# The maximum over 128 partitions taken on TensorE and VectorE instead of GpSimd, in a sparse attention with a mixture of experts

## The chip, the cores and the metric

The kernel runs on one core of a Trainium2 chip. A core has TensorE (PE in the profile, with its weight loads as PEld), VectorE (DVE), ScalarE (ACT), GpSimd (POOL) and SyncE (SP, which here issues most DMAs). Data lies in SBUF, in 128 partitions; TensorE writes to PSUM, of 8 banks. The metric is the device time of one execution in microseconds, as the median of several runs.

## The reference

First a block-sparse attention for 4 batches, 8 heads, 768 positions and a head dimension of 64, then eight dense experts over the 3072 rows of 512 that come out of it, mixed by a matrix `P` that is normalised eight times over its rows and its columns. Cut to what matters:

```python
scores = np.where(mask, scale * q @ k.T, -1e9)       # mask by blocks of 32
attn = softmax(scores)
x = (attn @ v)  -> (3072, 512)

logits = x @ w_gate                                   # (3072, 8)
logits = logits - logits.max()                        # one maximum over all
P = np.exp(logits)
for _ in range(8):
    P /= P.sum(1, keepdims=True) + 1e-09
    P /= P.sum(0, keepdims=True) + 1e-09
    P *= N / E
for e in range(8):
    h = np.maximum(x @ w1[e], 0.0)                    # (512 x 1024)
    out += P[:, e:e+1] * (h @ w2[e])                  # (1024 x 512)
```

## The kernel before

**Numbers in two halves.** TensorE multiplies float16 here. Each float32 operand of an expert's product is split into a high and a low float16 part, and three products (high by low, low by high, high by high) are added up. Before the split an operand is multiplied by a power of two, made from the largest absolute value of the whole tensor. That maximum lies over all 128 partitions: VectorE first reduces each partition to one number, then the 128 numbers are reduced to one that every partition needs. The second step is the GpSimd library call `partition_all_reduce` (PARTITION_ALL_REDUCE in the profile). It is called for the gate's weights and for v of each batch (`pow2_scale`, L120), for w1 and w2 of each of the eight experts (`scale_steps`, L177), and for the maximum of the logits (`weigh`, L897).

**Attention.** The program text walks over 192 tiles of 128 rows (`T`). For each it makes scores (L510, L513), adds the mask and takes the row maximum (L518), exponentiates (L523), splits the result in two halves (L532, L536; some on POOL), has a DMA turn it (`pt<-ph`, L558), and four tile pairs later multiplies by v (L577, into one of two PSUM banks called "pm", which one head's sums hold for six tiles). v is loaded, scaled and split per batch. The first expert's w1 is scaled in this stage too.

**Experts.** A step `i` is one expert and one batch, 32 in all. `stage1(i, qi)` makes a quarter of the hidden layer by a scheme of seven block products instead of eight (L945, into one of four banks "ph"); DVE combines the products (L955), ACT and POOL form sums (`add`, L1010 to L1022, with four POOL pieces at L1017 and L843), and the results are split into `h` (ACT L965, DVE or POOL L975). `stage2(i, p)` multiplies by w2 (L1058, into four banks "py") and DVE adds to the output (L1079). Step `i`'s second stage and step `i + 1`'s first alternate on PE.

**A new expert.** When the last batch of an expert is at work, the next expert's w1 is split into seven operands (ACT L821, DVE L825), with sums of its blocks formed on POOL (L836). Only then is the one raw buffer `r` free, and w2 is loaded into it (2 MB, L156), scanned for its maximum in eight parts (`part`, L170), reduced (`whole`, L176), passed to the library call (L177), turned into a scale (`power`, L180 to L185), and split, again with sums on POOL (L836). One batch later the w1 of the expert after that is loaded and scanned in the same way.

**What sets the order.** A class `Slots` holds these side jobs in the program text: urgent ones and a lazy list, the latter strictly in its order. After each product PE is given, `tick` advances the clock of the list by one and takes the next jobs that are due and that fit beside PE by their costs. `scale_w` puts the eight parts, `whole` and `power` on the lazy list:

```python
slots.add(whole, key, 1, True, dve=0.1)
slots.add(power, key, 2, True, dve=0.5)
```

The text's order is not the last word: at build time the instructions of all engines are ordered again by a model of their times, so that the scan of the first w1, for instance, which the text has at tile 101 of 192, runs 118 us after the start. Each engine then works through its own queue in order.

Of the kernel before, what the change touches and what calls it, by code (L numbers as in the profile page):

```python
# [8 lines left out]

# [1 line left out]
F32 = mybir.dt.float32  # L11
# [5 lines left out]
ALU = mybir.AluOpType  # L17
AX = mybir.AxisListType
PSUM = bass.MemoryType.PSUM

P = 128
# [25 lines left out]
TW = 100  # L47
# [12 lines left out]
def tile_sparse_attention_moe(  # L60
# [11 lines left out]
    nc = tc.nc  # L72
    B, H, S, D = q.shape
    NT, DM = out.shape
    NE, _, FF = w1.shape
# [20 lines left out]
    ident = const.tile([P, P], F32, name="ident")  # L96
# [3 lines left out]
    lg = const.tile([P, NTT, NE], F32, name="lg")  # L100
# [6 lines left out]
    dram = ctx.enter_context(tc.tile_pool(name="dram", bufs=1, space=bass.MemoryType.DRAM))  # L107
    xd = [dram.tile([P, NP, 2, KH, TH], F16, name=f"xd_{b}") for b in range(B)]

    def pow2_scale(srcs, s, inv, tag):  # L110
        m = small.tile([P, len(srcs)], F32, tag="mx", name=f"mx_{tag}")
        for i, src in enumerate(srcs):
            nc.vector.tensor_reduce(
                out=m[:, i : i + 1], in_=src, axis=AX.X, op=ALU.max, apply_absolute_value=True
            )
        if len(srcs) > 1:
            nc.vector.tensor_reduce(out=m[:, 0:1], in_=m, axis=AX.X, op=ALU.max)
        m = m[:, 0:1]
        a = small.tile([P, 1], F32, tag="ma", name=f"ma_{tag}")
        nc.gpsimd.partition_all_reduce(a, m, P, ReduceOp.max)  # L120
        nc.vector.tensor_scalar(a, a, TINY, HUGE, ALU.max, ALU.min)
        ai = a.bitcast(I32)
        nc.vector.tensor_scalar(ai, ai, 0x7F800000, None, ALU.bitwise_and)
        nc.vector.reciprocal(s, a)
        nc.vector.tensor_scalar(s, s, TOP, None, ALU.mult)
        nc.vector.tensor_scalar(inv, a, 1.0 / TOP, None, ALU.mult)
# [23 lines left out]
    wr = {}  # L150
# [5 lines left out]
        nc.sync.dma_start(out=t, in_=src[e].rearrange("(c p) f -> p c f", p=P))  # L156
        wr[which] = t

    def scale_steps(which, e, vector=nc.vector, gpsimd=nc.gpsimd):
        flat = wr[which].rearrange("p c f -> p (c f)")  # L160
        n = 8
        w = KD * FF // n
        m = small.tile([P, n], F32, tag="mx", name=f"mx_w{which}_{e}")
        a = small.tile([P, 1], F32, tag="ma", name=f"ma_w{which}_{e}")
        s = small.tile([P, 1], F32, tag=f"sw{which}", name=f"sw{which}_{e}")
        inv = small.tile([P, 1], F32, tag=f"iw{which}", name=f"iw{which}_{e}")
        wr["s", which], wr["i", which, e] = s, inv

        def part(k):
            vector.tensor_reduce(  # L170
                out=m[:, k : k + 1], in_=flat[:, k * w : (k + 1) * w], axis=AX.X,
                op=ALU.max, apply_absolute_value=True,
            )

        def whole():
            vector.tensor_reduce(out=a, in_=m, axis=AX.X, op=ALU.max)  # L176
            gpsimd.partition_all_reduce(a, a, P, ReduceOp.max)  # L177

        def power():
            vector.tensor_scalar(a, a, TINY, HUGE, ALU.max, ALU.min)  # L180
            ai = a.bitcast(I32)
            vector.tensor_scalar(ai, ai, 0x7F800000, None, ALU.bitwise_and)
            vector.reciprocal(s, a)
            vector.tensor_scalar(s, s, TOP, None, ALU.mult)
            vector.tensor_scalar(inv, a, 1.0 / TOP, None, ALU.mult)  # L185

        return [lambda k=k: part(k) for k in range(n)], whole, power

    KB = 1024
    w1p = {  # L190
# [127 lines left out]
    with ExitStack() as actx:  # L318
# [18 lines left out]
        with tc.tile_pool(name="mk", bufs=1, side="right") as mk:  # L337
            sbi = mk.tile([P, NB * NR], I64, name="sbi")
            nc.scalar.dma_start(
                out=sbi[R],  # L340
# [23 lines left out]
                out=sb[R],  # L364
# [51 lines left out]
        ps_t = pool("ps_t", 2, space=PSUM)  # L416
        ps_m = pool("ps_m", 2, space=PSUM)
        bank = [lambda nm: ps_m.tile([P, 512], F32, tag="pm", name=nm)]

        qscale = 1.0 / 8.0  # L420
        LDQ = (nc.sync, nc.gpsimd, nc.scalar)[QSEL]
# [216 lines left out]
        parts = {}  # L638
        ready, rest = first_steps()
        for T in range(NTILE + 4):  # L640
            if T < NTILE:
                parts[T] = front(T)
                if T + 1 < NC:
                    lay_mask(T + 1)
            if 0 <= T - LHI < NTILE:
                split_hi(T - LHI, *parts[T - LHI])
            if 0 <= T - LLO < NTILE:
                split_lo(T - LLO, *parts.pop(T - LLO))
                if (T - LLO) % G == G - 1:
                    transposes((T - LLO) // G)  # L650
            if T >= NTILE:
                continue
            if T // G >= LAG and T < NTILE and T % G == VPOS:
                for ci in range(G):
                    values(T // G - LAG, ci)
            n, c = divmod(T, NC)
            b, h = divmod(n, H)
            if n % 2 == 0 and c == CL and n // 2 + 2 < B * NHP:
                load_qk(*divmod(n // 2 + 2, NHP))
            if T == 20:  # L660
                split_gate()
            if T == 1:
                prep_q(1)
            if T == 2:
                prep_k(1)
                vsplit[0] = scale_v(0)
            if T in (3, 4, 5, 6):
                split_v(2 * T - 6, *vsplit[0])
            if todo and T % 3 == 0:
                todo.pop(0)()  # L670
            while ready and ready[0][0] <= T:
                ready.pop(0)[1]()
                if T % 2 == 0:
                    break
            if T == TW:
                load_w(1, 0)
                parts_w, whole_w, power_w = scale_steps(1, 0)
            if T - TW in range(1, 9):
                parts_w[T - TW - 1]()
            if T == TW + 10:  # L680
                whole_w()
            if T == TW + 12:
                power_w()
            if T < NTILE:
                if n + AHEAD < B * H:
                    if c == CQ:
                        prep_q(n + AHEAD)
                    if c == CK:
                        prep_k(n + AHEAD)
                if b + 1 < B:  # L690
                    if (h, c) == (2, 0):
                        load_v(b + 1)
                    if (h, c) == (3, 5):
                        vsplit[b + 1] = scale_v(b + 1)
                    if h >= 4 and c == 5:
                        split_v(2 * (h - 4), *vsplit[b + 1])
# [47 lines left out]
    ]  # L744
    accs = {b: big.tile([P, NC, DM], F32, name=f"acc_{b}") for b in range(B // 2)}
    bank[0] = lambda nm: ps_y.tile([P, 512], F32, tag="py", name=nm)

    def acc(t):
        return accs[t // NC][:, t % NC]
# [8 lines left out]
    class Slots:  # L758
        def __init__(self):
            self.now, self.pe, self.busy = 0, 0.0, [0.0, 0.0, 0.0]  # L760
            self.urgent, self.lazy = [], []

        def add(self, fn, key, delay=1, lazy=False, dve=0.0, act=0.0, pool=0.0):
            queue = self.lazy if lazy else self.urgent
            queue.append((fn, key, self.now + delay, (dve, act, pool)))

        def charge(self, costs):
            self.busy = [x + c for x, c in zip(self.busy, costs)]

        def run(self, queue, n):  # L770
            fn, _, _, costs = queue.pop(n)
            self.charge(costs)
            fn()

# [6 lines left out]
        def tick(self, pe, dve, act=0.0):  # L781
            self.now += 1
            self.pe += pe
            self.busy = [max(x, self.pe - lag) for x, lag in zip(self.busy, LAGS)]
            self.charge((dve, act, 0.0))
            n, held = 0, set()
            while n < len(self.urgent):
                _, key, ready, costs = self.urgent[n]
                if key not in held and ready <= self.now and self.fits(costs):
                    self.run(self.urgent, n)  # L790
                    n, held = 0, set()
                    continue
                held.add(key)
                if key[0][0] == "sum":
                    held.update((("h", key[1], p),) + key[1:] for p in (2, 4, 5, 6))
                n += 1
            while self.lazy and self.lazy[0][2] <= self.now and self.fits(self.lazy[0][3]):
                self.run(self.lazy, 0)

        def settle(self, i, qi):  # L800
            while any(x[1][1:] <= (i, qi) for x in self.urgent):
# [6 lines left out]

    slots = Slots()
    def scale_w(which, e):  # L810
        parts, whole, power = scale_steps(which, e, Pinned.vector, Pinned.gpsimd)
        key = ("scale", which, e)
        for k, part in enumerate(parts):
            slots.add(part, key, 6 if k == 0 else 1, True, dve=0.6)
        slots.add(whole, key, 1, True, dve=0.1)
        slots.add(power, key, 2, True, dve=0.5)

    def queue_split(dst, src, key, delay=1):
        s = wr["s", 1 if key[0] == "w1" else 2]
# [69 lines left out]
    def balance():  # L889
# [4 lines left out]

        def weigh():
            nc.vector.tensor_reduce(out=m, in_=flat(lg), axis=AX.X, op=ALU.max)
            nc.gpsimd.partition_all_reduce(m, m, P, ReduceOp.max)  # L897
            nc.vector.tensor_scalar(m, m, -1.0, None, ALU.mult)
            nc.scalar.activation(flat(pw), flat(lg), AF.Exp, bias=m)

# [304 lines left out]
```

## Time and profile before

| | |
|---|---|
| median of 3 runs | 2617.84 us |
| lowest and highest run | 2589.72 and 2622.93 us |
| the profiled execution | 2589.72 us, span 2589.7 us |
| attention | from 0 to some 612 us |
| first w2 loaded from | 606.9 us |
| later loads of w2 | 873.8, 1121.7, 1363.3, 1605.1, 1847.5, 2090.0, 2332.6 us |
| library calls | 22: 16 for w1 and w2, 4 for v, 1 for the gate, 1 for the logits |

The profiled execution is the lowest of the three. The loads of w2 mark the experts: from one to the next is an expert's period, 242 to 248 us. A profile row names the line and engine, what is written and read by the program's names, and how often; rows of the timeline begin with start and length in microseconds and end with the idle time before, and with the instruction that ended it. "Waits" rows give the total, the number of times and the longest.

### The profile page before, as it was taken

How to read it: one execution, taken by the hardware profiler on the slowest of the kernel's cores; microseconds unless marked ns; L12 is line 12 of the kernel's file. 1: busy time of each engine (PE TensorE's matmuls, PEld its weight loads, DVE VectorE, ACT ScalarE, POOL GpSimd, SP SyncE). 2: the span in 40 equal slices, each digit the busy share in tenths (PEclk: the TensorE clock that was granted, in tenths of full speed). 3: DMA queues.
4: the chain of work that ended last, by engine and by line, in shares of the span. 5: the costliest groups of instructions: out<-in, count | busy, mean ns of one | idle time of the engine just before them, and what ended most of it. 6: DMA issues, size and time to landing. Idle time of an engine off the chain costs nothing.

```text
span 2589.7 us, 46975 instructions
## 1 busy us (share of the span) xinstructions
PE 2361.4 (91%) x18270; PEld 1678.2 (65%) x18270; DVE 2009.5 (78%) x3747; ACT 1277.7 (49%) x2234; POOL 1559.8 (60%) x1387
## 2 busy tenths in 40 slices
PE   6999999897879979998998999899989998998999
PEld 3656666564656657765775677577657765776777
DVE  6768788675767788788778878877887788778876
ACT  4466767664445544444454444444444444444442
POOL 4557687763754476457556655755476557556653
PEclk9967879787989989999999999999999999999999
DMA  5679999996111221122121212211221122121211
GB/s 167 141 154 190 190 186 197 182 203 134 58 68 44 76 76 44 44 76 76 48 82 62 87 47 76 76 44 44 76 76 44 44 76 76 57 73 60 84 68 50
DMA packets 363924, 236.38 MB, mean 91 GB/s; under 512 B 303772, under 2 KB 316084, under 8 KB 363700
## 3 DMA queue, kind: packets, MB, share of 16 engines
q1 hardware_dynamic: 362128, 230.59, 34.9%
q10 hardware_dynamic: 1572, 2.78, 0.6%
q8 instruction: 143, 2.34, 0.4%
q14 instruction: 81, 0.66, 0.1%
HBM read 140.54 MB, written 17.30 MB: 61 GB/s over the span
## 4 chain that ended last, share of the span: by engine, by line
PE 59%; DVE 15%; POOL 9%; issue 8%; DMA 6%; ACT 2%; SPq 0%; DVEq 0%; POOLq 0%; ACTq 0%
PE py L1058 24%; PE p L945 22%; PE sc L513 4%; PE sc L510 4%; PE u L577 3%; DMA pt<-ph 3%; POOL r L836 3%; DMA r<-in_moe_w_dram 3%; DVE mx_w L170 2%; DVE h L975 2%; DVE acc L1079 2%; POOL h L975 2%; DVE w1p L825 1%; DVE u L955 1%; DVE a L955 1%
## 5 line engine op out<-in xcount | busy, mean ns | idle before, releaser
L1058 PE MATMUL py<-w2p,h 128*128 128x256 f16 x8064 | 974.6, 276 | 59.9 <-DVE acc L1079 21.3
L1058 PEld LDWEIGHTS <-h 128*128 128x128 f16 x8064 | 795.0, 99 | 221.6 <-issue 23.9
L1079 DVE SCALAR_TENSOR_TENSOR acc<-py,spare,acc 128x256 f32<-128x256 f32 (+1 forms) x840 | 457.8, 580 | 50.6 <-PE py L1058 49.4
L945 PE MATMUL p<-arena 128*128 128x384 f16 x2304 | 424.5, 334 | 70.9 <-DVE c L955 34.2
L975 POOL TENSOR_TENSOR h<-u,h 128x384 f16<-128x384 f32 x128 | 135.0, 1055 | 571.4 <-ACT h L965 474.2
L945 PEld LDWEIGHTS <-w1p 128*128 128x128 f16 x3072 | 302.5, 99 | 215.6 <-issue 41.5
L945 PE MATMUL p<-x,w1p 128*128 128x384 f16 x2304 | 407.4, 328 | 15.7 <-ACT a L990 13.3
L945 PEld LDWEIGHTS <-arena 128*128 128x128 f16 x2304 | 229.3, 100 | 213.1 <-issue 89.4
L965 ACT ACTIVATE h<-c 128x384 f16<-128x384 f32 x256 | 132.2, 522 | 351.8 <-DVE c L955 275.3
L536 POOL TENSOR_TENSOR ph<-pe,ph 128x768 f16<-128x768 f32 x144 | 259.8, 1818 | 69.1 <-ACT ph L532 51.9
L518 DVE CUSTOM_DVE_ANT_0 pe<-sc,mask 128x768 f32<-128x768 f32 x192 | 182.6, 954 | 112.3 <-PE sc L513 92.1
L955 DVE SCALAR_TENSOR_TENSOR a<-p,a 128x384 f32<-128x384 f32 x384 | 210.7, 549 | 20.2 <-PE p L945 15.0
L523 ACT ACTIVATE pe<-pe,nm 128x768 f32<-128x768 f32 x192 | 174.9, 928 | 98.6 <-DVE nm L522 86.2
L510 PE MATMUL sc<-k,q 128*128 128x512 f32 (+1 forms) x384 | 199.2, 519 | 18.8 <-DVE nm L518 17.2
L513 PE MATMUL sc<-k,q 64*128 64x512 f32 (+1 forms) x384 | 200.8, 524 | 0.0
L965 ACT ACTIVATE h<-r 128x384 f16<-128x384 f32 x256 | 132.2, 521 | 97.9 <-POOL r L843 94.3
L1017 POOL TENSOR_TENSOR s<-a,u 128x384 f32<-128x384 f32 x128 | 141.0, 1101 | 51.0 <-ACT a L1014 51.0
L577 PE MATMUL u<-vh,pt 128*128 128x66 f16 x2304 | 149.3, 211 | 17.8 <-DMA pt<-ph 16.9
L843 POOL TENSOR_TENSOR r<-s,r 128x384 f32<-128x384 f32 x128 | 149.0, 1164 | 23.6 <-issue 14.0
L945 PE MATMUL p<-arena,w1p 128*128 128x384 f16 x768 | 149.5, 330 | 14.9 <-DVE a L955 9.6
L577 PEld LDWEIGHTS <-pt 128*128 128x128 f16 x3456 | 140.1, 109 | 30.4 <-DMA pt<-ph 18.7
L843 POOL TENSOR_TENSOR c<-c,r 128x384 f32<-128x384 f32 x128 | 149.5, 1168 | 9.2
(155 smaller groups left out, 3439.7 us busy)
## 6 DMA issues: line engine op xcount, KB each, us to landing
arena<-xd SPq DMA_DIRECT2D x124, 384.0 KB, 3.8
x<-xd SPq DMA_DIRECT2D x93, 384.0 KB, 4.1
r<-in_moe_w_dram SPq DMA_DIRECT2D x16, 2048.0 KB, 8.8
arena<-in_q_dram SPq DMA_DIRECT2D x16, 384.0 KB, 3.5
arena<-in_k_dram SPq DMA_DIRECT2D x16, 384.0 KB, 4.1
arena<-in_v_dram SPq DMA_DIRECT2D x4, 1536.0 KB, 8.6
xd<-xs_t SPq DMA_DIRECT2D x16, 384.0 KB, 3.0
out_dram<-acc SPq DMA_DIRECT2D x24, 256.0 KB, 2.0
```

The costliest lines, as they stand in the source:

```text
L510: nc.tensor.matmul(sc[:, lo:hi], lhsT=q1[:, qc], rhs=k1[:, lo:hi], start=True, stop=False)
L513: nc.tensor.matmul(sc[:, lo:hi], lhsT=q2[:D, qc], rhs=k1[:D, lo:hi], start=False, stop=True)
L518: nc.vector.tensor_tensor_reduce(out=pe, in0=sc[:, :S], in1=masks[c], scale=1.0, scalar=-FMAX, op0=ALU.add, op1=ALU.max, accum_out=nm,)
L536: eng.tensor_tensor(out=lo, in0=pe, in1=hi, op=ALU.subtract)
L577: nc.tensor.matmul(uv[:, c], lhsT=a[:, ci * NC + kc, :], rhs=w[:, h, kc, :], start=(kc == 0 and m == 0), stop=(kc == NC - 1 and m == 2),)
L843: nc.gpsimd.tensor_tensor(out=out, in0=x, in1=y, op=ALU.subtract)
L945: nc.tensor.matmul(ps, lhsT=w1p[p][:, l, kc, fs], rhs=xp[p][:, r, kc], start=(kc == 0 and m == 0), stop=(kc == KH - 1 and m == 2),)
L955: nc.vector.scalar_tensor_tensor(out=t, in0=ps, scalar=HDOWN, in1=other, op0=ALU.mult, op1=ALU.add)
L965: nc.scalar.activation(h[:, 0], src, AF.Relu if relu else AF.Copy)
L975: eng.tensor_tensor(out=h[:, 1], in0=src, in1=h[:, 0], op=ALU.subtract)
L1058: nc.tensor.matmul(py, lhsT=hs[i, p, kc][:, l, tsl], rhs=w2p[p][:, r, kc], start=(kc == 0 and m == 0), stop=(kc == KF // 2 - 1 and m == 2),)
L1079: nc.vector.scalar_tensor_tensor(out=dst, in0=src, scalar=c, in1=dst, op0=ALU.mult, op1=ALU.add)
```

## The change

All calls of the library are taken out. Where the 128 numbers were reduced, TensorE now transposes a matrix whose 128 columns are all the same column: every partition of the result holds all 128 numbers, in PSUM, and VectorE takes the maximum along the row. The bank for it is one of "pm" in attention, and one of "ph" (shared with the first stage's products) among the experts.

```diff
+    spread_bank = [None]
+
+    def spread_max(a, tag):
+        ps = spread_bank[0](f"all_{tag}")
+        nc.tensor.transpose(
+            out=ps[:, :P], in_=a[:, 0:1].to_broadcast([P, P]), identity=ident
+        )
+        return ps[:, :P]
+
     def pow2_scale(srcs, s, inv, tag):
...
-        nc.gpsimd.partition_all_reduce(a, m, P, ReduceOp.max)
+        nc.vector.tensor_reduce(out=a, in_=spread_max(m, tag), axis=AX.X, op=ALU.max)
...
         def whole():
             vector.tensor_reduce(out=a, in_=m, axis=AX.X, op=ALU.max)
-            gpsimd.partition_all_reduce(a, a, P, ReduceOp.max)
+
+        def spread():
+            wr["all", which] = spread_max(a, f"w{which}_{e}")
 
         def power():
+            vector.tensor_reduce(out=a, in_=wr["all", which], axis=AX.X, op=ALU.max)
             vector.tensor_scalar(a, a, TINY, HUGE, ALU.max, ALU.min)
...
+        spread_bank[0] = bank[0]
...
             if T == TW + 10:
                 whole_w()
+            if T == TW + 11:
+                spread_w()
             if T == TW + 12:
                 power_w()
...
+    spread_bank[0] = lambda nm: ps_h.tile([P, 512], F32, tag="ph", name=nm)
...
             while self.lazy and self.due(self.lazy[0]):
                 self.run(self.lazy, 0)
+
+        def due(self, item):
+            _, _, ready, costs, gap = item
+            return max(ready, self.last + gap) <= self.now and self.fits(costs)
...
         slots.add(whole, key, 1, True, dve=0.1)
-        slots.add(power, key, 2, True, dve=0.5)
+        slots.add(spread, key, 1, True, gap=2)
+        slots.add(power, key, 1, True, dve=0.8, gap=2)
...
         def weigh():
             nc.vector.tensor_reduce(out=m, in_=flat(lg), axis=AX.X, op=ALU.max)
-            nc.gpsimd.partition_all_reduce(m, m, P, ReduceOp.max)
+            nc.vector.tensor_reduce(out=m, in_=spread_max(m, "lg"), axis=AX.X, op=ALU.max)
```

`last` is the tick at which a lazy job last ran, so a `gap` of 2 keeps a job two ticks behind the one before it: `spread` two ticks after `whole`, and `power` two after `spread`.

More of the change, by code (lines that the diff above doesn't have):

```diff
@@ L5 @@
 from concourse import mybir
-from concourse.bass_isa import ReduceOp
 from concourse.masks import make_identity
@@ L157, in load_w, with scale_steps @@
         wr[which] = t
-    def scale_steps(which, e, vector=nc.vector, gpsimd=nc.gpsimd):
+    def scale_steps(which, e, vector=nc.vector):
         flat = wr[which].rearrange("p c f -> p (c f)")
@@ L185, in power @@
             vector.tensor_scalar(inv, a, 1.0 / TOP, None, ALU.mult)
-        return [lambda k=k: part(k) for k in range(n)], whole, power
+        return [lambda k=k: part(k) for k in range(n)], whole, spread, power
     KB = 1024
@@ L676, in tile_sparse_attention_moe @@
                 load_w(1, 0)
-                parts_w, whole_w, power_w = scale_steps(1, 0)
+                parts_w, whole_w, spread_w, power_w = scale_steps(1, 0)
             if T - TW in range(1, 9):
@@ L761, in __init__, with add @@
             self.urgent, self.lazy = [], []
-        def add(self, fn, key, delay=1, lazy=False, dve=0.0, act=0.0, pool=0.0):
+            self.last = 0
+        def add(self, fn, key, delay=1, lazy=False, dve=0.0, act=0.0, pool=0.0, gap=0):
             queue = self.lazy if lazy else self.urgent
-            queue.append((fn, key, self.now + delay, (dve, act, pool)))
+            queue.append((fn, key, self.now + delay, (dve, act, pool), gap))
         def charge(self, costs):
@@ L770, in run @@
         def run(self, queue, n):
-            fn, _, _, costs = queue.pop(n)
+            fn, _, _, costs, _ = queue.pop(n)
+            if queue is self.lazy:
+                self.last = self.now
             self.charge(costs)
@@ L787, in tick @@
             while n < len(self.urgent):
-                _, key, ready, costs = self.urgent[n]
+                _, key, ready, costs, _ = self.urgent[n]
                 if key not in held and ready <= self.now and self.fits(costs):
@@ L796, in tick @@
                 n += 1
-            while self.lazy and self.lazy[0][2] <= self.now and self.fits(self.lazy[0][3]):
+            while self.lazy and self.due(self.lazy[0]):
                 self.run(self.lazy, 0)
+        def due(self, item):
+            _, _, ready, costs, gap = item
+            return max(ready, self.last + gap) <= self.now and self.fits(costs)
         def settle(self, i, qi):
@@ L810, in scale_w @@
     def scale_w(which, e):
-        parts, whole, power = scale_steps(which, e, Pinned.vector, Pinned.gpsimd)
+        parts, whole, spread, power = scale_steps(which, e, Pinned.vector)
         key = ("scale", which, e)
```

## The prediction

> **What bounds the kernel now.** I read the head of the page, then the work by stage, then the stages' own waits.
>
> ```profile
> span 2589.7 us, 46975 instructions
> PE 2361.4 (91%) x18270; PEld 1678.2 (65%) x18270; DVE 2009.5 (78%) x3747; ACT 1277.7 (49%) x2234; POOL 1559.8 (60%) x1387
> PE 59%; DVE 15%; POOL 9%; issue 8%; DMA 6%; ACT 2%; SPq 0%; DVEq 0%; POOLq 0%; ACTq 0%
> ```
>
> TensorE (PE) is busy 91% of the span and carries 59% of the chain that ended last. GpSimd (POOL) carries only 9%, but 8% of the chain, some 207 us, is "issue": time in which an engine waited for nothing that the profile shows.
>
> The windows view, by stage (columns: length, then PE, PEld, DVE, ACT, POOL busy, the granted TensorE clock, DMA share, GB/s):
>
> ```profile
> 50.00:600.00 550.00, 514.75 (x4589) 335.28 (x4588) 409.79 (x907) 358.65 (x505) 375.41 (x258) 0.83 0.94 181
> 615.00:873.80 258.80, 212.38 (x1524) 149.49 (x1522) 187.82 (x357) 125.94 (x237) 142.32 (x129) 0.90 0.19 61
> 873.80:1121.60 247.80, 225.73 (x1662) 163.84 (x1660) 192.99 (x336) 113.44 (x212) 144.62 (x139) 0.97 0.18 62
> 1605.10:1847.50 242.40, 225.00 (x1680) 164.94 (x1680) 195.59 (x342) 109.45 (x206) 145.41 (x139) 0.99 0.19 64
> ```
>
> Attention has the DMA engines at 0.94 and PE busy 515 of 550 us; there is little room beside these two. The experts are another matter. An ordinary one (1605 to 1848) has 17 us without PE work, the one before 1122 has 22, the first 46. So the question is which of those gaps belong to the GpSimd library call. The POOL timeline shows its two calls of one expert, for w2 (1625) and for the next w1 (1692), with the work on either side (start, length, instruction, idle before):
>
> ```profile
> 1625.19 0.38 POOL L177 PARTITION_ALL_REDUCE ma_w<-ma_w  x1 [8.60 <-DVE ma_w L176]
> 1632.50 1.24 POOL L975 TENSOR_TENSOR h<-u,h 128x384 f16<-128x384 f32 x1 [6.92 <-ACT w2p L821]
> 1633.70 1.97 POOL L1017 TENSOR_TENSOR s<-a,u 128x384 f32<-128x384 f32 x1
> ...
> 1639.26 3.41 POOL L836 TENSOR_TENSOR r<-r 128x256 f32<-128x256 f32 x4
> ...
> 1684.89 1.23 POOL L975 TENSOR_TENSOR h<-c,h 128x384 f16<-128x384 f32 x1
> 1692.05 0.38 POOL L177 PARTITION_ALL_REDUCE ma_w<-ma_w  x1 [5.93 <-issue]
> 1699.30 0.90 POOL L975 TENSOR_TENSOR h<-u,h 128x384 f16<-128x384 f32 x1 [6.87 <-ACT a L990]
> ```
>
> The call is written as 0.38 us, but POOL does nothing for 5.93 us before it and 6.87 us after it: 13.2 us from 1686.1 to 1699.3. The releaser printed behind the second gap isn't its cause: 6.92 us behind one call and 6.87 behind the other are put down to two different pieces of ACT's work. The sequencer's row says what lies there:
>
> ```profile
> L177 POOLq MODIFY_POOL_CONFIG  x30: 1/8/18, 630.8 to 2344.6; - x30
> L177 POOL PARTITION_ALL_REDUCE ma_w<-ma_w x16: 377/378/423, 133.0 to 2351.8; - x16
> ```
>
> With the four calls for v, one for the gate and one for the logits there are 22 calls; two pairs stand side by side, so 20 gaps of about 13 us.
>
> By the Trainium skill, "GPSIMD Engine Reference", section Instruction dispatch, it is the first call of a freshly loaded routine that pays about 6 us for loading; this trace agrees on the 6 us, but shows it twice, and at every call. By the page's one load the change would be worth some 6 us in all, not what follows.
>
> **The change, part by part.** All 22 calls go and with them the gaps. What that is worth is read from who waited.
>
> *Ordinary experts (2 to 7, six pairs of calls).* The longest of PE's waits, the rows that hold it and the next, and what stands behind it:
>
> ```profile
> PE p L945 <- DVE c L955: 5.3, 2, 5.1
> 1656.37 2.08 PE L945 MATMUL p<-arena 128*128 128x384 f16 x6 [5.12 <-DVE c L955]
> 1659.85 1.14 PE L945 MATMUL p<-arena 128*128 128x384 f16 x6
> 1693.13 1.61 PE L945 MATMUL p<-arena 128*128 128x384 f16 x6 [2.30 <-DVE u L955]
> 1655.75 0.56 DVE L955 SCALAR_TENSOR_TENSOR c<-p,u 128x384 f32<-128x384 f32 x1 [0.88 <-POOL s L1017]
> 1628.99 0.52 ACT L1014 ACTIVATE a<-a 128x384 f32<-128x384 f32 x1 [1.94 <-DVE a L955]
> ```
>
> PE's 5.12 us at 1656 hang on DVE's `c`, which hangs on POOL's `s`, which stands behind POOL's queue of w2 sums (L836), begun at 1639.26. That queue began late because four pieces of `add` stood first, from 1633.70. Their input `a` was there at 1629.5; without the reload they run from then, 4.2 us earlier, and so do the sums. I take 4 of the 5.12 us. After the wait six matmuls take 2.08 us and a little later 1.14: the clock has fallen and comes back, 1.5 us in all with the pieces between. The w1 call stops DVE at L180 until 1692.4, and PE for 2.30: I take 2, and 0.5 for the slower matmuls (1.61 against 1.14). Together 8.0.
>
> What is added, by the nearest rows:
>
> ```profile
> L604 PE MATMUL xt<-ident,xn 128*128 128x128 f32 x96 | 18.4, 343 | 0.0
> L170 DVE TENSOR_REDUCE mx_w<-r 128x1 f32<-128x512 f32 x128 | 78.6, 675 | 14.4 <-DMA r<-in_moe_w_dram 14.4
> L176 DVE TENSOR_REDUCE ma_w<-mx_w 128x1 f32<-128x8 f32 x16 | 2.3, 146 | 0.0
> ```
>
> A 128x128 transpose in float32 is 0.34 us, a reduction over 128 elements 0.27 us (146 ns plus 120 of the 504 further elements that cost 529 ns). Two of each per pair, on engines that are late there: 1.2 us. Net 6.8, times six: **41 us**. The bounds: 8 if the 4 and the 1.5 stay (six times 2.5 - 1.2), 57 if all of 5.12 and 2.30 and 2 of clock go and the added work hides beside other work.
>
> Two waits are added. The transpose waits on PE for DVE's `whole` (L176); behind it on PE's queue stand the products (L945) and L1058, and DVE's combinations (L955) wait for those. The reduction in `power` waits on DVE for the transpose; behind it stand L955 and L1079. The slots leave two ticks between the steps, each a product or more of PE's work (six matmuls, 1.14 us at 1659.85). I take the waits at nothing, with these ticks as cover, and price them under the rivals. The transpose also holds one of four "ph" banks for two ticks, in which two products take two others. Four ticks, some 4.6 us, now lie between `whole` and the scale, where the call stood; at worst the split of w2 starts that much later, and then the 4 us are lost again, which is the lower bound above.
>
> *Experts 0 and 1.* PE's own rows around the calls at 636, 699 and 734 (the logits' maximum), and PE's waits from 874 to 1122:
>
> ```profile
> 637.56 4.00 PE L945 MATMUL p<-arena 128*128 128x384 f16 x12 [4.92 <-DVE ma_w L182]
> 646.77 2.08 PE L945 MATMUL p<-arena,w1p 128*128 128x384 f16 x6 [5.22 <-DVE sw L184]
> 700.96 1.14 PE L945 MATMUL p<-arena 128*128 128x384 f16 x6 [2.16 <-DVE c L955]
> 735.07 5.26 PE L1058 MATMUL py<-w2p,h 128*128 128x256 f16 x34 [7.83 <-DVE h L975]
> 744.20 0.39 PE L1058 MATMUL py<-w2p,h 128*128 128x256 f16 x2 [3.88 <-ACT h L965]
> 746.45 0.39 PE L1058 MATMUL py<-w2p,h 128*128 128x256 f16 x1 [1.85 <-DVE h L969]
> PE p L945 <- DVE a L955: 8.4, 2, 6.8
> PE p L945 <- ACT a L990: 4.2, 1, 4.2
> ```
>
> Here the gaps lie bare. Of 10.1 us at 637 and 647 I take 7 (the weights' split follows at once), of 2.2 at 701 2, of 13.6 from 735 to 746 11 (transpose and reduction stay), and 3 for the clock after them: **23 us**, between 12 (half) and 29 (all). Of 6.8 and 4.2 in expert 1 I take **8**, between 3 and 11.
>
> *Attention.* The chain in order of time has, around the first calls and the last:
>
> ```profile
> 22.97 1.98 issue
> ...
> 25.73 6.90 issue
> ...
> 257.70 4.19 issue
> ```
>
> That is 13.1 us; at 133 the chain runs through PE and the call costs nothing. Since DMA at 0.94 is next late, I take **6**, between 0 and 13. The transpose there takes one of two "pm" banks, which the value sums hold for several tiles; its cover is the other bank, and no row bounds it but PE's own waits, so it stays within these 6.
>
> The sum: 41 + 23 + 8 + 6 = 78 us. The profiled execution took 2589.72 us, which is its span, and is the lowest of the three runs; the median lies 28 us above it. So 2512 on its own scale, and 2540 on the median's.
>
> **The rivals.** *All of it comes back.* 57 + 29 + 11 + 13 = 110 us, 2508; if what else PE waits in an ordinary expert (17.4 less the 7.4 counted) shrinks by a third, another 20: 2488. For it: POOL's 260 us of gaps (20 times 13) are far more than I count. Against it: DVE has 195 of 242 us in an expert and w2 must still be loaded and scanned.
>
> *The sums weren't last.* If DVE or the loading of w2, and not POOL's queue, sets the steps after 1640, the 5.1 us stay. Then 8 + 3 + 16 (expert 0 without its first 7) + 6 = 33 us, 2585. For it: the 8.60 us before the w2 call were a wait for DVE, which no edit takes away.
>
> *PE waits for DVE's maximum: slower.* POOL stood 8.60 us for L176 at 1625. If PE reaches its transpose as early, it idles as long, and everything in its queue with it. At the 14 calls for the weights of experts 1 to 7 that is 120 us against the 78 gained: 42 us slower, 2660. It decides from 78 / 14 = 5.6 us a call. For it: the wait of 8.60. Against it: the two ticks, and the bare 5.1 us at 1656, which show PE's queue held by DVE too, so PE isn't ahead by so much.
>
> *The gaps are hidden anyway.* Then only the added 22 times 0.6 us count: 13 us slower, 2631. Against it: DVE's and PE's waits above. By the Trainium skill, "GPSIMD Engine Reference", section Engine selection, a reduction over partitions belongs on GpSimd and not on VectorE, which would speak for this case; the 0.38 us of the call alone agrees with the page, the gaps around it don't.
>
> That a library call stays behind would show in MODIFY_POOL_CONFIG; all 40 stand at the three lines removed, so I give this no weight.
>
> **How the numbers follow.** Forecast (2508 to 2575) 0.55, all back 0.17, sums not last 0.18, PE waits 0.06, hidden 0.04. The likeliest gives 2540. Without the two slow cases and the far ends of the others, 2480 to 2605 holds about 8 in 10; that includes some 15 us either way because the compiled order of all engines is drawn up anew. The measurement tells about 2% from no change, so faster means below 2565: the forecast but for its upper end, and all back, 0.70. Within 2% lie the sums-not-last case, hidden, most of PE waits, and that end: 0.26. Slower: 0.04.
>
> **What would show it.** No PARTITION_ALL_REDUCE and no MODIFY_POOL_CONFIG; POOL starting `add` right after ACT's L1014 in the w2 scan, and the sums some 4 us sooner; PE's wait for `c` near 1 us, 2.3 for `u` gone; an ordinary expert near 235.6 us, the first some 23 us shorter. I am wrong if PE shows waits of several us at the transpose, if the expert keeps 242 us with the same wait for `c`, or if attention, at the same DMA share, grows.

## The result, and the profile after

| | before | after |
|---|---|---|
| median | 2609.16 us (4 runs) | 2499.44 us (4 runs) |
| lowest and highest | 2589.72 and 2622.93 | 2476.73 and 2510.40 |
| profiled execution's span | 2589.7 | 2503.9 |

The ratio is 0.960, with a 95% interval of 0.952 to 0.967: 105 us faster by the ratio, 86 us between the two profiled executions (that of the kernel before is the fastest of its four runs, that of the changed kernel the third of its four). Measured again beside another kernel, the ratio was 0.964 (0.960 to 0.968), or 93 us.

The head of the page of the changed kernel (L numbers are now its own: products L968, `py` L1081, `h` L998, combinations L978, `s` L1040, sums L859):

```profile
span 2503.9 us, 46982 instructions
PE 2352.3 (94%) x18292; PEld 1680.1 (67%) x18292; DVE 2044.1 (82%) x3769; ACT 1279.7 (51%) x2234; POOL 1551.4 (62%) x1365
PE 59%; DVE 16%; POOL 9%; issue 7%; DMA 5%; ACT 2%; DVEq 0%; POOLq 0%; ACTq 0%; SPq 0%
```

POOL has 22 instructions less, PE and DVE have 22 more each. The windows view shows where the time went (attention, then three periods from one load of w2 to the next, the last an ordinary one; columns as before):

```profile
50.00:600.00 550.00, 513.57 (x4542) 336.33 (x4542) 418.21 (x912) 352.69 (x499) 365.99 (x250) 0.78 0.91 177
608.40:840.40 232.00, 209.18 (x1649) 150.79 (x1647) 196.91 (x374) 131.45 (x249) 148.32 (x132) 0.99 0.24 78
840.40:1073.60 233.20, 222.14 (x1664) 163.00 (x1662) 194.99 (x339) 113.62 (x212) 146.02 (x137) 0.99 0.20 66
1543.40:1777.60 234.20, 223.27 (x1682) 164.36 (x1682) 198.82 (x344) 109.91 (x206) 145.23 (x137) 0.99 0.20 66
```

From the issue times of the w2 loads, which mark the experts (the first, the third and the last; the second is at 840.44):

```profile
608.39 0.57 SPq L164 DMA_DIRECT2D r<-in_moe_w_dram  x1
...
1073.59 0.38 SPq L164 DMA_DIRECT2D r<-in_moe_w_dram  x1
...
2247.78 0.38 SPq L164 DMA_DIRECT2D r<-in_moe_w_dram  x1
```

| stretch | before | after | gain | predicted |
|---|---|---|---|---|
| attention, to the first w2 load | 606.9 | 608.4 | -1.5 | 6 |
| expert 0 | 266.9 | 232.1 | 34.9 | 23 |
| expert 1 | 247.8 | 233.2 | 14.7 | 8 |
| experts 2 to 6, each | 242.19 | 234.84 | 7.35 | 6.8 |
| from the last load to the end | 257.1 | 256.1 | 1.0 | 6.8 |

The sum of the gains is 86, that of the prediction 78. But one row stands out: the last stretch has a w2 call and no w1 call, and gained 1 us only.

### The profile page after: what moved, and what is told of

Its sections match the earlier page's. It is cut to its first block, busy times and chain, and to the rows that moved or that the text cites. A ratio compares the mean times of both kernels' runs of the same rounds, so it can differ in the third digit from the quotient of the medians.

```text
span 2503.9 us, 46982 instructions
## 1 busy us (share of the span) xinstructions
PE 2352.3 (94%) x18292; PEld 1680.1 (67%) x18292; DVE 2044.1 (82%) x3769; ACT 1279.7 (51%) x2234; POOL 1551.4 (62%) x1365
## 4 chain that ended last, share of the span: by engine, by line
PE 59%; DVE 16%; POOL 9%; issue 7%; DMA 5%; ACT 2%; DVEq 0%; POOLq 0%; ACTq 0%; SPq 0%
PE py L1081 23%; PE p L968 22%; PE sc L525 4%; PE sc L522 4%; PE u L589 4%; POOL r L859 3%; DMA r<-in_moe_w_dram 2%; DVE h L998 2%; DMA pt<-ph 2%; DVE mx_w L178 2%; POOL h L998 2%; DVE u L978 2%; DVE acc L1102 2%; DVE w1p L848 1%; DVE a L978 1%
## 5 line engine op out<-in xcount | busy, mean ns | idle before, releaser
L1081 PE MATMUL py<-w2p,h 128*128 128x256 f16 x8064 | 971.1, 275 | 61.6 <-ACT h L988 23.9
L1081 PEld LDWEIGHTS <-h 128*128 128x128 f16 x8064 | 790.2, 99 | 219.0 <-ACT h L988 28.8
L998 POOL TENSOR_TENSOR h<-u,h 128x384 f16<-128x384 f32 x128 | 126.9, 992 | 603.0 <-ACT h L988 603.0
L968 PEld LDWEIGHTS <-w1p 128*128 128x128 f16 x3072 | 303.0, 99 | 199.0 <-issue 26.1
L968 PE MATMUL p<-x,w1p 128*128 128x384 f16 x2304 | 417.1, 330 | 14.1 <-DVE r L978 11.8
L968 PE MATMUL p<-arena 128*128 128x384 f16 x2304 | 404.9, 326 | 14.9 <-DVE a L978 9.9
L968 PEld LDWEIGHTS <-arena 128*128 128x128 f16 x2304 | 225.2, 98 | 149.5 <-issue 19.5
L978 DVE SCALAR_TENSOR_TENSOR a<-p,a 128x384 f32<-128x384 f32 x384 | 210.8, 549 | 18.4 <-PE p L968 14.2
L1040 POOL TENSOR_TENSOR s<-a,u 128x384 f32<-128x384 f32 x128 | 130.4, 1019 | 70.9 <-ACT a L1037 70.8
L589 PE MATMUL u<-vh,pt 128*128 128x66 f16 x2304 | 153.6, 214 | 17.8 <-DMA pt<-ph 17.6
L589 PEld LDWEIGHTS <-pt 128*128 128x128 f16 x3456 | 145.3, 111 | 29.4 <-DMA pt<-ph 19.8
L866 POOL TENSOR_TENSOR r<-s,r 128x384 f32<-128x384 f32 x128 | 154.7, 1209 | 9.6
L522 PEld LDWEIGHTS sc<-k,q 128*128 128x128 f32 x384 | 87.2, 228 | 96.0 <-issue 70.4
```

The lines of the kernel that those rows point to most:

```text
L522: nc.tensor.matmul(sc[:, lo:hi], lhsT=q1[:, qc], rhs=k1[:, lo:hi], start=True, stop=False)
L589: nc.tensor.matmul(uv[:, c], lhsT=a[:, ci * NC + kc, :], rhs=w[:, h, kc, :], start=(kc == 0 and m == 0), stop=(kc == NC - 1 and m == 2),)
L866: nc.gpsimd.tensor_tensor(out=out, in0=x, in1=y, op=ALU.subtract)
L968: nc.tensor.matmul(ps, lhsT=w1p[p][:, l, kc, fs], rhs=xp[p][:, r, kc], start=(kc == 0 and m == 0), stop=(kc == KH - 1 and m == 2),)
L978: nc.vector.scalar_tensor_tensor(out=t, in0=ps, scalar=HDOWN, in1=other, op0=ALU.mult, op1=ALU.add)
L998: eng.tensor_tensor(out=h[:, 1], in0=src, in1=h[:, 0], op=ALU.subtract)
```

## The experiments

**Attention alone, and all but attention.** `lib_experts` keeps the new way in attention and puts the library call, in its old slots, back for w1, w2 and the logits; `lib_attention` does the reverse. The edits are the lines of the change taken back at those places.

```diff
 # lib_experts
+        lib = (which == 1 and e > 0) or which == 2
...
+            if lib:
+                nc.gpsimd.partition_all_reduce(a, a, P, ReduceOp.max)
...
+        if (which == 1 and e > 0) or which == 2:
+            slots.add(power, key, 2, True, dve=0.5)
 # lib_attention, in pow2_scale (and for e == 0 of w1)
+        nc.gpsimd.partition_all_reduce(a, m, P, ReduceOp.max)
```

> The new way in attention only (v, gate, first w1); the library call stays for the experts' w1 and w2 and for the logits, in its old slots. If attention gives the 6 us of the prediction: about 2603 against 2609 before, ratio 0.998, and expert periods of 242 us as before. If the 20 us by which the median of the change moved further than its profiled execution (105 against 86 us) come from attention: about 2585, ratio 0.991. If attention gives nothing, since its DMA engines are next late: 1.000.

> The reverse: the library call in attention only, the new way in the experts and for the logits. If attention gives 6 us: about 2505, ratio 0.962, expert periods of 234 to 235 us as in the changed kernel. If attention gives 20: about 2520, ratio 0.968. The two halves should add up to the whole, 105 us.

Measured: `lib_experts` 2600.22 us, ratio 0.998 (0.994 to 1.002) to the kernel before; `lib_attention` 2505.48 us, ratio 0.964 (0.960 to 0.968). The experts and the logits carry the whole gain. For attention the 6 us are as possible as nothing; 20 us aren't.

**A library call that nobody waits for.** `idle_call` is the changed kernel with 15 more library calls, on each maximum, into a column that nothing reads:

```diff
             vector.tensor_reduce(out=a, in_=m, axis=AX.X, op=ALU.max)
+            if (which, e) != (1, 0):
+                idle = small.tile([P, 1], F32, tag="idle", name=f"idle_w{which}_{e}")
+                nc.gpsimd.partition_all_reduce(idle, a, P, ReduceOp.max)
```

> The changed kernel with 15 extra library calls in the experts: GpSimd also reduces each w1's and w2's maximum, into a column that nothing reads. Theory A (GpSimd's own gaps cost the time, since add's pieces stand behind them): the gaps of 13 us come back and with them most of the time, periods near 241 us and some 2570 to 2590, ratio 0.985 to 0.993. Theory B (what cost the time was VectorE standing at the answer, L180): nobody waits for this answer, periods stay near 235 us, 2500 to 2510, ratio 0.96.

Measured: 2617.76 us, ratio 1.008 (1.004 to 1.011): all of the gain is gone, and 0.8% more. Theory B falls; VectorE waits for no answer here. The timeline of its POOL, DVE and PE around the w1 call of an ordinary expert:

```profile
1724.53 0.38 POOL L188 PARTITION_ALL_REDUCE idle_w<-ma_w  x1 [6.06 <-PE p L972]
1732.08 0.90 POOL L1002 TENSOR_TENSOR h<-c,h 128x384 f16<-128x384 f32 x1 [7.17 <-issue]
...
1733.82 0.98 POOL L1044 TENSOR_TENSOR s<-a,u 128x384 f32<-128x384 f32 x1
...
1735.39 0.90 DVE L1002 TENSOR_TENSOR h<-s,h 128x384 f16<-128x384 f32 x1 [10.69 <-ACT h L992]
...
1736.82 2.08 PE L972 MATMUL p<-x,w1p 128*128 128x384 f16 x6 [9.69 <-DVE a L982]
```

The gaps of 6 and 7 us stand around the call as before, POOL's next `h` comes 13 us later, and PE stands 9.69 us for DVE's `a`, with nothing in the kernel that uses the call's result. The chain between them is in the rows: POOL's `s` comes only at 1733.8, ACT's `h` needs `s`, DVE stands 10.69 us for that `h`, and DVE's `a` is next in its queue. It is the idle POOL itself that costs, and here it costs more than theory A asked for (ratio 0.985 to 0.993): the ordinary expert lasts 248.8 us, against 242.2 in the kernel before and the 241 of theory A.

**The same order without the library.** `plain_op` is the kernel before with an ordinary GpSimd instruction on the same column in place of each call. It leaves out the maximum over the partitions.

```diff
-            gpsimd.partition_all_reduce(a, a, P, ReduceOp.max)
+            gpsimd.tensor_scalar(a, a, 1.0, 1.0, ALU.mult, ALU.mult)
```

> The kernel before with each library call replaced by an ordinary GpSimd instruction on the same column; the maximum over the partitions is left out, so each partition scales by its own. Everything else, the wait for GpSimd's answer too, stays. If only the changing of the library costs, this is as fast as the changed kernel or faster by the price of its transposes and reductions (7 to 13 us): 2490 to 2500, ratio 0.955 to 0.96, periods 234 or less. If the later start of w2's split, which the changed kernel shows (power 20 us after whole), is itself a part of the gain, this one is slower: periods 237 to 240 us, 2520 to 2550, ratio 0.966 to 0.977.

Measured: 2481.28 us, ratio 0.954 (0.950 to 0.958). Its ordinary expert, by the loads of w2, POOL at the two places where the calls were, the start of its w2 sums, and PE's longest wait:

```profile
1041.88 0.38 SPq L156 DMA_DIRECT2D r<-in_moe_w_dram  x1
...
1512.38 0.38 SPq L156 DMA_DIRECT2D r<-in_moe_w_dram  x1
...
2217.83 0.38 SPq L156 DMA_DIRECT2D r<-in_moe_w_dram  x1
...
1532.41 0.19 POOL L177 TENSOR_SCALAR ma_w<-ma_w 128x1 f32<-128x1 f32 x1 [8.55 <-DVE ma_w L176]
...
1542.99 3.74 POOL L836 TENSOR_TENSOR r<-r 128x256 f32<-128x256 f32 x4
...
1590.48 0.18 POOL L177 TENSOR_SCALAR ma_w<-ma_w 128x1 f32<-128x1 f32 x1
1597.77 1.17 POOL L975 TENSOR_TENSOR h<-u,h 128x384 f16<-128x384 f32 x1 [7.11 <-ACT h L965]
...
1560.75 2.02 PE L945 MATMUL p<-arena 128*128 128x384 f16 x6 [3.19 <-DVE c L955]
```

(2217.83 - 1041.88) / 5 = 235.19 us, against 234.84 in the changed kernel. So among the ordinary experts the transposes and reductions and the later scale together cost nothing that shows. Two profiles of the changed kernel differ by 0.9 us in this period (234.84 and, for `after_again` below, 233.97), so less than that can't be told. What `plain_op` has beyond the changed kernel lies ahead of them: its first w2 is loaded at 575.5 us instead of 608.4.

The POOL rows also say how much of a gap was the library's. Without it POOL still stands 8.55 us before the w2 instruction, for DVE's maximum, and 7.11 us behind the w1 instruction, for ACT's `h`. From POOL's work before the w1 call to its work after it pass 13.2 us in the kernel before and 7.3 here; at the w2 call 15.9 and 10.1. So in an ordinary expert each call kept POOL idle for some 6 us longer, not for 13.

**One call at a time.** `w1_new` has the library for w2 alone, `w2_new` for the experts' w1 alone (edits as in `lib_experts`, with one condition each).

> The changed kernel with the library call put back for w2 alone (8 calls, in their old slots); w1, the logits and attention keep the new way. By the prediction's steps w1's call gives 2.5 us less 0.6 of an ordinary expert, so its period is 240.3 us against 242.2 before, and the whole about 2555, ratio 0.98. By what the two traces show (the last expert, which has a w2 call and no w1 call, came out only 1.0 us shorter, the ordinary ones 7.4) w1's call gives 6.3: period 235.9, the whole about 2525, ratio 0.968.

> The reverse: the library call for the experts' w1 alone (7 calls); w2 keeps the new way. By the prediction's steps w2's call gives 5.5 us less 0.6: period 237.3. By the two traces it gives 1.0: period 241.2, the whole about 2550, ratio 0.975. If the two calls are one cause together (POOL is late as long as one of them is left), both this and the kernel with w1 alone stay near 240.

Measured: `w1_new` 2550.94 us, ratio 0.983 (0.978 to 0.988); `w2_new` 2569.45, ratio 0.989 (0.984 to 0.995). The loads of w2 (first `w1_new`, then `w2_new`), and PE's longest wait of an ordinary expert in each (in the second one at the w1 call):

```profile
1095.83 0.38 SPq L165 DMA_DIRECT2D r<-in_moe_w_dram  x1
...
2287.32 0.38 SPq L165 DMA_DIRECT2D r<-in_moe_w_dram  x1
...
1624.91 2.08 PE L977 MATMUL p<-arena 128*128 128x384 f16 x6 [5.13 <-DVE c L987]
```

```profile
1093.47 0.38 SPq L165 DMA_DIRECT2D r<-in_moe_w_dram  x1
...
2314.70 0.38 SPq L165 DMA_DIRECT2D r<-in_moe_w_dram  x1
...
1679.69 2.08 PE L977 MATMUL p<-arena 128*128 128x384 f16 x6 [4.00 <-DVE ma_w L199]
```

The periods are 238.30 and 244.25 us. Neither reading held: not the prediction's 240.3 and 237.3, nor that of the last stretch (235.9 and 241.2). The calls don't add up, as six kernels together show. The new way for w2 also moves the split of w2 later (next part):

| ordinary expert, us | no gap | w1's gap | w2's gap | both |
|---|---|---|---|---|
| w2 split early | 235.2 (`plain_op`) | not run | 238.3 (`w1_new`) | 242.2 (before) |
| w2 split late | 234.8 (after) | 244.2 (`w2_new`) | not run | 248.8 (`idle_call`) |

(In `idle_call` nobody waits for the answers, in the others DVE does.) With the early split w2's gap costs 3.1 us and w1's 3.9 on top; with the late one w1's costs 9.4 and w2's 4.6 on top. So a gap has no price of its own in these six kernels; it depends on the order around it. (The 3.1 and the 3.9 are not far enough apart to rank them, with 0.9 us between two profiles of one kernel.) PE's waits in the 30 us from the start of w1's gap show the difference: 2.3 us in the kernel before, 6.7 in `w2_new`, 9.7 in `idle_call`. Why the late split makes w1's gap dearer isn't shown: the w2 sums end some 3 us ahead of the gap in either order (at 1683.7 with the gap from 1686.1 in the kernel before, at 1669.0 with the gap from 1672.5 in `w2_new`).

**The ticks between the steps.** `gap0` takes the two gaps out.

```diff
-        slots.add(spread, key, 1, True, gap=2)
-        slots.add(power, key, 1, True, dve=0.8, gap=2)
+        slots.add(spread, key, 1, True)
+        slots.add(power, key, 1, True, dve=0.8)
```

> The changed kernel without the two ticks between whole, the transpose and power (gap 0 for both). The rival of the prediction, that PE stands at its transpose for VectorE's maximum: PE waits of several us at L113 and an ordinary expert 5 us or more longer than 234.8; at 14 calls some 2560 to 2580, ratio 0.98 to 0.99. If VectorE is early enough anyway (in the changed kernel whole was done 17.7 us before the transpose): no wait at L113, period 233 to 236, ratio 0.957 to 0.963.

Measured: 2510.38 us, ratio 0.968 (0.962 to 0.973), period 234.32. The ratio lies within the interval of the changed kernel measured again (0.960 to 0.968). PE doesn't wait for the maximum at the transposes, with or without the ticks: its waits at L113 come to 1.2 us over all 22, none of them for it (this row is of `gap0`; a wait would stand at its end):

```profile
1343.35 0.27 PE L113 MATMUL all_w<-ident,ma_w 128*128 128x128 f32 x1
```

**The logits' call alone.** `lib_logits` puts the library back at L920 only.

```diff
-            nc.vector.tensor_reduce(out=m, in_=spread_max(m, "lg"), axis=AX.X, op=ALU.max)
+            nc.gpsimd.partition_all_reduce(m, m, P, ReduceOp.max)
```

> The changed kernel with the library call put back for the logits' maximum alone, one call in expert 0. By the prediction it is worth 11 us of waits and part of 3 us of clock: expert 0 lasts some 245 us from one load of w2 to the next, against 232.0 changed and 266.9 before. If the clock, which was granted at 0.88 around this call before and at 1.00 now, is worth more: 250 or above. The whole is 10 to 20 us above the changed kernel.

Measured: 2507.63 us (2 runs), ratio 0.966 (0.959 to 0.974); expert 0 lasts 249.9 us against 232.1. By this one profile, a single call among 22 costs 17.8 us; the medians can't confirm it, since 0.966 from 2 runs lies within that same interval. PE's waits behind it:

```profile
710.60 2.08 PE L969 MATMUL p<-x,w1p 128*128 128x384 f16 x6 [6.75 <-DVE a L979]
...
721.71 0.39 PE L1082 MATMUL py<-w2p,h 128*128 128x256 f16 x2 [3.00 <-ACT h L989]
723.21 0.40 PE L1082 MATMUL py<-w2p,h 128*128 128x256 f16 x1 [1.11 <-DVE h L993]
```

These are 10.9 us. PE's busy time in expert 0 is 216.4 us against 209.2 in the changed kernel, so most of the other 7 are slower matmuls.

**The bank in attention.** `pt_bank` takes the transposes' bank in attention from the pair "pt"; `after_again` is the changed kernel beside it on the same chip.

```diff
-        spread_bank[0] = bank[0]
+        spread_bank[0] = lambda nm: ps_t.tile([P, 512], F32, tag="pt", name=nm)
```

> The changed kernel with one edit: in attention the transpose's bank is one of the two 'pt' banks (turned q and k) instead of one of the two 'pm' banks (the value sums). With plain_op attention was done at 576 us, with every kernel that has either the library or the transpose there at 603 to 621. Theory P, the bank holds the transposes back (gate and v) and with them the split of v: attention ends at 575 to 590, the whole 15 to 30 us below the changed kernel, ratio about 0.99 to it. Theory Q, attention is bound by DMA and by the granted clock and its length is a matter of how the compiled order falls: 600 to 620, no difference from the changed kernel beyond 0.5%.

> The changed kernel once more beside the one with the other bank, on the same chip: as before, ratio 0.96 to the kernel before, experts of 234 to 235 us, and attention ending within some 5 us of 608 if its length belongs to the compiled order; 595 to 620 if it belongs to the execution.

Measured: `pt_bank` 2494.12 us, ratio 0.958 (0.955 to 0.962) to the kernel before; `after_again` 2506.62, 0.964 (0.960 to 0.968). It is 12.5 us, or 0.5%, below the changed kernel and the fastest of the complete kernels, though the two intervals overlap a little. The gate's transpose in the changed kernel and in `pt_bank`:

```profile
97.55 0.32 PE L113 MATMUL all_g<-ident,mx_g 128*128 128x128 f32 x1
```

```profile
66.11 0.42 PE L113 MATMUL all_g<-ident,mx_g 128*128 128x128 f32 x1
```

Its input was ready at 15.7 and 15.9 us; it stands 31 us earlier in the second, and the first w2 is loaded at 583.4 us against 615.8 in `after_again` (and 608.4 in the first profile of that same kernel, so some 7 us of this belong to the execution). Expert 0 gives 12.8 of these 32 us back (244.6 against 231.8). Attention fits theory P, the whole gains less than the 15 to 30 us it named, and the compiled order of all of attention differs too: that it was the bank that did it isn't shown.

## Why the prediction was right, and where it wasn't

The direction, the time (2540 forecast, 2480 to 2605 as the range, 2499 measured) and the main mechanism held: the library call costs by the gaps around it, not by its 0.38 us (`idle_call`, `plain_op`). No PARTITION_ALL_REDUCE and no MODIFY_POOL_CONFIG is left. The 78 us were low, by 8 against the two profiles and by 15 to 27 against the two ratios. Step by step:

**Added work: right.** The rows after:

```profile
L113 PE MATMUL all_w<-ident,ma_w x16: 272/273/457, 367.9 to 2285.4; 128*128 128x128 f32 x16
L190 DVE TENSOR_REDUCE ma_w<-all_w x16: 276/282/292, 372.4 to 2288.2; 128x1 f32<-128x128 f32 x16
```

0.27 and 0.28 us, where 0.34 and 0.27 were taken. The 1.2 us per pair that I charged don't show in the period (234.84 against 235.19 in `plain_op`).

**Ordinary experts: right sum, wrong parts, so the sum is partly luck.** I took 4 of the 5.12 us at `c` because the w2 sums would start 4.2 us sooner. `plain_op`, with the order kept and the gaps gone, is the test: its sums start 30.6 us after the load instead of 34.1, so 3.5 sooner, but PE's wait only falls to 3.19. The step that failed is the conversion of an earlier start into a shorter wait; 1.9 came, not 4. The products that wait for `c` start 2.9 us sooner after the load (48.4 instead of 51.3), and PE reaches them about 1 us sooner as well, which leaves 1.9. The w1 call, at 2.5, was priced too low (3.9 in the table above, more with the late split), and the w2 call, at 5.5, too high (3.1): 7.0 together for the 8.0 of the sum, because the two errors have opposite signs.

In the changed kernel itself the sums didn't start sooner at all. From `whole` to the scale, which I set at four ticks or 4.6 us, pass 20.4 us (POOL, then DVE and PE of an ordinary expert after; w2 loaded at 1543.35):

```profile
1564.94 0.91 POOL L998 TENSOR_TENSOR h<-u,h 128x384 f16<-128x384 f32 x1 [10.12 <-ACT h L988]
1567.76 1.00 POOL L1040 TENSOR_TENSOR s<-a,u 128x384 f32<-128x384 f32 x1 [1.91 <-ACT a L1037]
...
1591.00 5.37 POOL L859 TENSOR_TENSOR r<-r 128x256 f32<-128x256 f32 x4
```

```profile
1563.14 0.14 DVE L184 TENSOR_REDUCE ma_w<-mx_w 128x1 f32<-128x8 f32 x1
...
1583.72 0.28 DVE L190 TENSOR_REDUCE ma_w<-all_w 128x1 f32<-128x128 f32 x1
```

```profile
1580.96 0.27 PE L113 MATMUL all_w<-ident,ma_w 128*128 128x128 f32 x1
...
1615.43 3.63 PE L1081 MATMUL py<-w2p,h 128*128 128x256 f16 x17 [3.19 <-ACT h L988]
```

`whole` is done at 1563.3, the transpose runs at 1581.0, the sums begin at 1591.0: 47.7 us after the load, 13.5 later than before. I had written that such a delay would lose the 4 us again. It lost nothing: `add` (`s` at 1567.8) runs undisturbed, and the sums find a free POOL later, at the price of a 3.19 us wait at 1615 in place of the 5.12. The waits for `c` and `u` are 0.2 us each, as I had asked for, but by another order than the one I gave as the reason. Over experts 2 to 6 PE's idle time fell by 6.6 us each (17.2 to 10.6) and its busy time by 0.7. `gap0` shows that the two ticks aren't the reason for the delay (its transpose still comes 35.3 us after the load, against 37.6). Most likely DVE gets `whole` earlier than its place in the text, and PE, always busy, its transpose at its own place; no run tested that.

**The last stretch: counted wrongly.** I took six pairs of calls, but the last expert has no w1 call. From the last load to the end pass 254.8 to 257.0 us in the eight profiles without a library call for w2, and 257.1, 258.1 and 260.1 in the kernel before, `w1_new` and `idle_call`. So the 1.0 us is a small price for the w2 call, seen through a spread of 2 us.

**Experts 0 and 1: too low, in expert 0 by the clock.** In expert 0 PE's idle time fell by 23.6 us (46.4 to 22.8), where I took 20; the clock behind the waits was the larger error. Two windows of expert 0, before and after:

```profile
606.90:674.50 67.60, 49.70 (x343) 31.43 (x341) 42.51 (x68) 32.12 (x60) 45.42 (x41) 0.80 0.29 89
674.50:760.00 85.50, 63.01 (x475) 44.04 (x476) 56.41 (x113) 32.59 (x65) 46.62 (x42) 0.88 0.22 76
```

```profile
608.40:671.70 63.30, 54.02 (x407) 35.31 (x406) 52.25 (x84) 39.27 (x75) 53.61 (x48) 0.97 0.30 95
671.70:757.00 85.30, 76.38 (x655) 58.27 (x654) 78.30 (x162) 36.57 (x72) 51.51 (x46) 1.00 0.21 76
```

The granted clock was 0.80 and 0.88 and is 0.97 and 1.00. Over the whole expert PE now needs 209.2 us of busy time instead of 220.5, for 17 matmuls more: 11.3 us, where I took 3. `lib_logits` agrees with the size: 11 us of waits at the logits, as predicted, 7 us of slower matmuls, and 17.8 us in all. In expert 1, 8 us were taken; PE's idle time fell by 11.0 (22.1 to 11.1) and its busy time by 3.6 (225.7 to 222.1), which I had not charged there.

**Attention: not resolved.** 6 us were predicted; -1.5 was seen in the profiles, and 0.998 (0.994 to 1.002) covers both. The start did gain, and behind it the clock was lower (first 50 us and the next, before and after):

```profile
0.00:50.00 50.00, 28.58 (x65) 12.54 (x65) 31.83 (x70) 19.62 (x31) 22.38 (x31) 1.00 0.45 146
50.00:100.00 50.00, 50.00 (x288) 30.74 (x287) 29.05 (x70) 24.41 (x33) 22.54 (x18) 1.00 0.69 149
```

```profile
0.00:50.00 50.00, 38.78 (x117) 18.95 (x117) 35.69 (x76) 25.87 (x39) 26.23 (x33) 1.00 0.69 194
50.00:100.00 50.00, 47.91 (x341) 29.70 (x341) 33.31 (x81) 28.32 (x42) 24.80 (x19) 0.80 0.73 138
```

PE does 10 us more work in the first 50 us; then its clock is 0.80 where it was 1.00. From 50 to 570 us it is 0.76 against 0.84. That this took the gain back is likely, not shown: `plain_op` has 0.78 there and still ends attention earlier. That DMA leaves little room there was too strong: `plain_op` and `pt_bank` end attention 25 to 33 us sooner than the changed kernel did in its first profile.

**The rivals.** "PE waits for DVE's maximum" fell: no wait for it at L113, not even in `gap0`. "The gaps are hidden anyway" can hold in attention only, where `lib_experts` doesn't tell 6 us from nothing. "The sums weren't last" was half right: with the gaps gone 3.19 of the 5.12 us stay. "All of it comes back" (2508, or 2488 with its extra 20) came nearest to the median of 2499, but that is luck: in an ordinary expert 7.35 us came back where it asked for 9.4, and what makes up for it is the clock in experts 0 and 1 and the choice of runs.

## What to carry to other kernels

When an engine's instruction looks cheap, read the idle time on both sides of it: here 0.38 us stood in 13.2 us without work. Then ask how long the engine would have waited there anyway: without the library 7.3 of these 13.2 us stayed. Price such a gap by the queue behind it at that place; a gap cost 3 to 18 us here, and two of them don't add up. Where a wait of PE goes, count the clock that it costs afterwards too.

## What the runs showed of the hardware

- Around a library call POOL does nothing for 5.8 to 6.0 us before it and 6.7 to 7.1 after it in the kernel before, wherever it has no longer wait for another engine (7.4 to 8.6 before most calls for w2 and the one for the logits). In `idle_call`, where nothing reads the result, it is 5.6 to 6.1 and 6.7 to 7.5.
- After a wait of PE of several us its matmuls run slower for a time: six took 2.08 us after 9.69 of waiting, against 1.14. In that place of `idle_call` the granted clock is 1.00 until 1730 us, 0.50 from 1732 to 1740 and 1.00 again from 1742, in windows of 2 us; PE waited from 1727.1 to 1736.8. By the Trainium skill, "TensorE: Matmul & The Clock Gate", Part 1, the clock falls to half after an idle window of about 3.4 us and needs as long to recover; the trace agrees on the half and, with 1.00 again 3 to 5 us after PE began anew, on the recovery, but a wait of less than 3.4 us was enough here: six matmuls took 2.02 us after 3.19 of waiting (`plain_op`) and 1.61 after 2.30 (the kernel before).
- In attention the granted clock from 50 to 570 us is 0.84 and 0.81 in the two kernels with library calls there (the kernel before and `lib_attention`), and 0.71 to 0.78 in nine without. In the five of them that were read in windows of 1 us, these are means of two values, 1.00 and 0.50, that take turns. The low one can hold for 36 us in which PE is busy all the time, as in the changed kernel:

```profile
155.00:191.00 36.00, 36.00 (x203) 22.72 (x202) 19.14 (x46) 20.42 (x29) 19.28 (x14) 0.50 0.64 123
```

So a wait of PE doesn't explain it, and the quick recovery of the experts isn't seen there; why it holds wasn't settled.
